# Seeding partial sums in PSUM by ScalarE copies in a two-layer Strassen-type matmul chain

## The chip, the cores and the metric

One core of a Trainium2 chip runs the whole program. The metric is device time in microseconds (us) of one execution; the kernel before takes 843.44 us (median of 3 runs, 843.13 to 844.32).

## What is computed

A decayed linear attention, then two feed-forward layers on the same 3072 tokens:

```python
for t in range(S):                                     # per batch b and head h, d = e = 64
    state = gamma * state + outer(k[t], v[t])
    y[t] = scale * q[t] @ state
x  = y.reshape(3072, 512)
x  = ((x @ w1) * (x @ w2)) @ w3 @ w_out                # w1, w2: 512x1024, w3: 1024x1024, w_out: 1024x512
x  = maximum(maximum(x @ w1', x @ w2'), x @ w3') @ w_out'   # w1' to w3': 512x768, w_out': 768x512
```

## The kernel before

The program has five stages, one behind the other, on TensorE (PE): attention (to 88 us), the products with w1 and w2 (called stage b here, 88 to 319 us), w3 merged with w_out and applied (to 494 us), the three products and their maximum (stage h, 494 to 760 us), and the last matrix. Its engines run instruction streams in a written order; nothing reorders them. VectorE is DVE, ScalarE ACT, GpSimd POOL, SyncE SP.

Stage b and stage h cut each matrix product into 2x2 quarters and form the four output quarters from seven products, q0 to q6, of summed quarters. Stage b runs 6 blocks: two groups `g` of weights times three blocks `n` of tokens (`blk = 3*g + n`). Stage h runs 9 blocks (`blk = 3*j + n`). In a block each product q makes GA = 4 (stage b) or GH = 3 (stage h) output pieces p, each of six matmuls into one PSUM bank of 512 columns. The seven products use two sets of banks, "a" and "b", by the table `ORDER`: q0 starts set a, q1 starts set b, q2 adds to a, q3 starts b anew, q4 adds to a, q5 adds to b, q6 adds to a. The sets change roles from block to block: set a of block n+1 is set b of block n.

After each piece its bank is read out (lines 494 to 511, 727 to 744): q0 is copied by ACT to the SBUF tile U, q1 is added to U by DVE, q2 and q3 are copied by ACT to C and E, q4 is subtracted from E by DVE, q5 subtracted from C by DVE and (stage b) multiplied with U on POOL, q6 multiplied with E (stage b) or put into a maximum (stage h). In stage h q1 gives m11: DVE adds the first piece into m11 (line 742), and for the other two adds to U and then takes the maximum with m11 (lines 742, 744).

Beside this run, ahead of the matmuls of a product:

- `op_split` (lines 241 and 242): the operand tile of a later product is rounded to a high part by ACT and gets its low part from DVE. In group 0 of stage b it is made two products ahead, from sums of quarters that `op_pre` (lines 255 to 261) forms on DVE three products ahead. In group 1 the tiles come back from DRAM by DMAs that ACT issues.
- `step`: the weights of the next group arrive as 64-bit numbers and are decoded in steps. A step alternates between `decode_a` (ACT line 117, POOL line 119, DVE lines 140, 142 and, of the piece before, line 134) and `decode_b` (ACT line 149, then a new fetch). `Spread` deals out the steps over the pieces, through `side.tick()` after each piece.
- `wgen` in the last block of a group: it makes the seven weight tiles of the next group (lines 204 to 214).

Of the kernel before, what the change touches and what calls it, by code (L numbers as in the profile page):

```python
# [12 lines left out]
ALU = mybir.AluOpType  # L13
# [19 lines left out]
GA = 4  # L33
# [14 lines left out]
def fused_kernel(ctx: ExitStack, tc: tile.TileContext, ck, w12, w3t, wo1, w123, wo2, mask, gout, gch, kdec, out):  # L48
    nc = tc.nc
# [119 lines left out]
    def store(dst, src, wait=1):  # L169
        later.append([wait, dst, src])  # L170
# [24 lines left out]
    def wslot(q, n=1024):  # L195
        return w_t[q][:, :2 * n].rearrange("p (h n) -> p h n", h=2)
# [55 lines left out]
    def op_pre(n, q, quad, quiet=False):  # L252
        t, sub = t_buf(n), ALU.subtract
        if q == 2:
            nc.vector.tensor_tensor(out=quad(0, 0), in0=quad(0, 1), in1=quad(0, 0), op=sub)
            nc.vector.tensor_tensor(out=t, in0=quad(1, 1), in1=quad(0, 0), op=sub)
        elif q == 3:
            eng = nc.vector if quiet else nc.gpsimd
            eng.tensor_tensor(out=quad(0, 1), in0=quad(1, 1), in1=quad(0, 1), op=sub)
        elif q == 5:  # L260
            nc.vector.tensor_tensor(out=t, in0=t, in1=quad(1, 0), op=sub)
# [106 lines left out]
    def quad_b(n):  # L368
        return lambda k, e: xr_t[n][:, 2 * k:2 * k + 2, e, :]
# [5 lines left out]
    with tc.manual_schedule():  # L375
# [23 lines left out]
        for _ in range(WARM):  # L399
# [7 lines left out]
        side = Spread([step] * (4 * GA) + [drain] + [job for q in (0, 1, 5, 2) for job in wgen.jobs(q)],  # L407
                      2 * (last - 3))
# [36 lines left out]
        for g in range(KF // GA):  # L445
            if g == 0:
                wq += [lambda i=i, u=u: fetch_w12(i, u) for i in range(GA, KF) for u in range(2)]
                more(3)
                side = Spread([idle] * 7 + [step] * (4 * GA), 2 * 28 + 4)
            else:  # L450
                x_st.close()
                m_st, m_pl = stage_pool("m")
                wo1_sb = [m_pl.tile([P, 2, 512], F32R, name=f"wo1_{k}") for k in range(KF)]
                w3_sb = [m_pl.tile([P, 2, 512], F32R, name=f"w3_{k}") for k in range(8)]
                w3_sb += [op_t[k // 2][:, :].rearrange("p (u h n) -> p u h n", u=2, h=2)[:, k % 2] for k in range(8)]
                wq += [lambda k=k: fetch(wo1[k], None, wo1_sb[k][:, 0], wo1_sb[k][:, 1]) for k in range(KF)]
                wq += [lambda k=k: fetch(w3t[k // 2, k % 2], None, w3_sb[k][:, 0], w3_sb[k][:, 1])
                       for k in range(2 * KF)]
                more(3)
                side = Spread([idle] * 3 + [step] * 32, 3 * 28)  # L460
            wgen = weights(raw_quads(1024), 1024)
            for n in range(NB):
                blk = g * NB + n
                sets = sets_b(blk)
                for q in range(7):
                    s = 7 * blk + q
                    if g == 0:
                        for d in (3, 2):
                            t = s + d
                            if t < 7 * NB:  # L470
                                qd = quad_b(t // 7)
                                if d == 3:
                                    op_pre(t // 7, t % 7, qd, quiet=True)
                                else:
                                    op_split(t, op_src(t // 7, t % 7, qd))
                                    store(opsp[t // 7, t % 7], op_t[t % 4].bitcast(F32))
                        if s < 2:
                            store(opsp[0, s], op_t[s].bitcast(F32))
                        for job in late_w.pop(s, ()):
                            job()  # L480
                    t = s + 3
                    if 7 * NB <= t < 14 * NB:
                        nc.scalar.dma_start(out=op_t[t % 4].bitcast(F32), in_=opsp[t // 7 - NB, t % 7])
                    which, first = ORDER[q]
                    x = op_slot(s)
                    w = wslot(q).rearrange("p h (i k n) -> p h i k n", i=GA, k=2)
                    for p in range(GA):
                        ps = sets[which][p]
                        for k in range(2):
                            wh, wl = w[:, 0, p, k, :], w[:, 1, p, k, :]  # L490
                            nc.tensor.matmul(ps, wh, x[:, 0, k, :], start=first and k == 0, stop=False, skip_group_check=True)  # L491
                            nc.tensor.matmul(ps, wh, x[:, 1, k, :], start=False, stop=False, skip_group_check=True)  # L492
                            nc.tensor.matmul(ps, wl, x[:, 0, k, :], start=False, stop=k == 1, skip_group_check=True)  # L493
                        u, c, e = (part(nm, p) for nm in "UCE")
                        if q == 0:
                            nc.scalar.copy(out=u, in_=ps)  # L496
                        elif q == 1:
                            nc.vector.tensor_tensor(out=u, in0=u, in1=ps, op=ALU.add)
                        elif q == 2:
                            nc.scalar.copy(out=c, in_=ps)  # L500
                        elif q == 3:
                            nc.scalar.copy(out=e, in_=ps)  # L502
                        elif q == 4:
                            nc.vector.tensor_tensor(out=e, in0=ps, in1=e, op=ALU.subtract)
                        elif q == 5:
                            nc.vector.tensor_tensor(out=c, in0=c, in1=ps, op=ALU.subtract)  # L506
                            nc.gpsimd.tensor_tensor(out=c, in0=c, in1=u, op=ALU.mult)  # L507
                            store(fsp[n, 0, :, g * GA + p, :], c, 1)
                        else:
                            nc.vector.tensor_tensor(out=e, in0=e, in1=ps, op=ALU.mult)  # L510
                            store(fsp[n, 1, :, g * GA + p, :], e, 0)
                        side.tick()
                    stores()
                    if g == 0 and n == NB - 1:
                        if q == 0:
                            side.rest()
                            drain()
                        wgen(q)
            side.rest()
# [149 lines left out]
        for j in range(GH):  # L669
# [16 lines left out]
            for n in range(NB):  # L686
# [3 lines left out]
                for q in range(7):  # L690
# [26 lines left out]
                    which, first = ORDER[q]  # L717
                    x = quads4(gen_t[s - held] if held <= s < held + len(gen_t) else op_t[s % 4])
                    w = wslot(q, 256 * GH).rearrange("p h (i k n) -> p h i k n", i=GH, k=2)
                    for p in range(GH):  # L720
                        ps = sets[which][p]
                        for k in range(2):
                            wh, wl = w[:, 0, p, k, :], w[:, 1, p, k, :]
                            nc.tensor.matmul(ps, wh, x[:, 0, k, :], start=first and k == 0, stop=False, skip_group_check=True)  # L724
                            nc.tensor.matmul(ps, wh, x[:, 1, k, :], start=False, stop=False, skip_group_check=True)  # L725
                            nc.tensor.matmul(ps, wl, x[:, 0, k, :], start=False, stop=k == 1, skip_group_check=True)  # L726
                        u, c, e = (part(nm, p) for nm in "UCE")
                        if q == 0:
                            nc.scalar.copy(out=u, in_=ps)
                        elif q == 2:  # L730
                            nc.scalar.copy(out=c, in_=ps)
                        elif q == 3:
                            nc.scalar.copy(out=e, in_=ps)
                        elif q == 6:
                            if p:
                                nc.vector.tensor_tensor(out=m12, in0=m12, in1=ps, op=ALU.max)
                            else:
                                nc.scalar.copy(out=m12, in_=ps)
                        else:
                            m, v, (x0, x1), op = {1: (m11, u, (u, ps), ALU.add), 4: (m22, e, (ps, e), ALU.subtract),  # L740
                                                  5: (m21, c, (c, ps), ALU.subtract)}[q]
                            nc.vector.tensor_tensor(out=v if p else m, in0=x0, in1=x1, op=op)
                            if p:
                                nc.vector.tensor_tensor(out=m, in0=m, in1=v, op=ALU.max)
                        side.tick()
# [117 lines left out]
```

## Time and profile before

| | |
|---|---|
| Median of 3 runs | 843.44 us |
| The profiled execution | 843.5 us, of which the span from first to last instruction is 841.7 us |
| Busy share of the span | PE 99%, DVE 70%, ACT 43%, POOL 14% |
| Instructions | PE 4720 matmuls, DVE 725, ACT 560, POOL 121 |
| TensorE clock granted | 1.000 of full speed |

A row of the timeline tells the start and length of one instruction (or of several alike in a row, with their number), and in brackets how long the engine had been idle and what it then waited for. A matmul row lasts 0.39 us, but the next one starts 0.23 us after it: matmuls overlap, so waits of PE are best read from starts. The group rows (by line) give number, total busy time, mean length in ns, and the idle time ahead of the group.

### The profile page before, as it was taken

Reading aid. Unit: us, or ns where it says so; the run is one execution under the profiler, and the core shown is the slowest. Engines: PE = TensorE matmul, PEld = TensorE weight load, DVE = VectorE, ACT = ScalarE, POOL = GpSimd, SP = SyncE. Lnnn points to the kernel's source line nnn. Section 1 sums busy time; section 2 is a strip of 40 time slices with the busy share of each in tenths; the row PEclk is TensorE's granted clock in tenths of the full one; section 3 lists DMA queues with packets and bytes.
Section 4 is the critical chain, followed back from the end, with each engine's and each line's share of the span. In section 5 each row is a group of like instructions: output and inputs, shape, how many; then the busy total and the mean of one; then the engine's idle time right before and its main releaser. Section 6 shows DMA issues by size and latency. Waiting matters only on the chain.

```text
span 841.7 us, 12200 instructions
## 1 busy us (share of the span) xinstructions
PE 830.0 (99%) x4720; PEld 694.1 (82%) x4720; DVE 589.0 (70%) x725; ACT 365.5 (43%) x560; POOL 120.8 (14%) x121
## 2 busy tenths in 40 slices
PE   8999999999999999999999999999999999999998
PEld 8889888878888888888888888887888888888886
DVE  3898978898475756753574657678657665878793
ACT  2544455354434343633555453343333334335542
POOL 3444031302031322100201000200000010000000
PEclk9999999999999999999999999999999999999999
DMA  9998367759988967462495699829998899856522
GB/s 347 408 406 337 152 283 289 288 213 369 362 324 312 340 228 263 150 218 87 147 336 213 218 410 412 334 88 382 409 361 300 318 367 357 291 239 228 209 101 75
DMA packets 54634, 235.00 MB, mean 279 GB/s; under 512 B 6320, under 2 KB 6448, under 8 KB 39344
## 3 DMA queue, kind: packets, MB, share of 16 engines
q1 hardware_dynamic: 37728, 133.46, 40.8%
q10 hardware_dynamic: 16848, 100.76, 32.5%
q8 instruction: 37, 0.61, 0.3%
q14 instruction: 21, 0.17, 0.1%
HBM read 161.85 MB, written 72.35 MB: 278 GB/s over the span
## 4 chain that ended last, share of the span: by engine, by line
PE 74%; DVE 3%; DMA 2%; issue 1%; ACT 0%; ACTq 0%; DVEq 0%
PE bank L724 9%; PE bank L725 9%; PE bank L726 9%; PE bank L492 5%; PE bank L601 5%; PE bank L603 5%; PE bank L493 5%; PE bank L602 5%; PE bank L491 5%; PE bank L783 3%; PE bank L784 3%; PE bank L782 3%; PE bank L540 2%; PE bank L542 2%; PE bank L541 2%; DMA opsp<-op 1%
## 5 line engine op out<-in xcount | busy, mean ns | idle before, releaser
L724 PE MATMUL bank<-op,w 128*128 128x512 f32 x360 | 140.1, 389 | 0.3 <-DMA op<-opsp 0.3
L725 PE MATMUL bank<-op,w 128*128 128x512 f32 x360 | 140.2, 389 | 0.2 <-DVE op L242 0.2
L726 PE MATMUL bank<-op,w 128*128 128x512 f32 x360 | 140.1, 389 | 0.0
L491 PE MATMUL bank<-op,w 128*128 128x512 f32 x336 | 130.9, 390 | 1.0 <-DVE E L510 1.0
L492 PE MATMUL bank<-op,w 128*128 128x512 f32 x336 | 130.9, 390 | 1.0 <-DVE op L242 1.0
L493 PE MATMUL bank<-op,w 128*128 128x512 f32 x336 | 130.7, 389 | 0.0
L119 POOL TENSOR_SCALAR dec<-dec 128x512 f32<-128x512 f32 x64 | 47.5, 742 | 481.6 <-ACT dec L117 457.2
L724 PEld LDWEIGHTS bank<-op,w 128*128 128x128 f32 x360 | 67.6, 188 | 14.8 <-issue 0.7
L725 PEld LDWEIGHTS bank<-op,w 128*128 128x128 f32 x360 | 67.6, 188 | 14.5 <-DVE op L242 0.6
L726 PEld LDWEIGHTS bank<-op,w 128*128 128x128 f32 x360 | 67.6, 188 | 14.1
L491 PEld LDWEIGHTS bank<-op,w 128*128 128x128 f32 x336 | 63.1, 188 | 14.7 <-ACT U L496 1.4
L492 PEld LDWEIGHTS bank<-op,w 128*128 128x128 f32 x336 | 63.1, 188 | 14.4 <-DVE op L242 1.7
L602 PE MATMUL bank<-op,w 128*128 128x512 f32 x192 | 74.7, 389 | 0.0
L601 PE MATMUL bank<-op,w 128*128 128x512 f32 x192 | 74.7, 389 | 0.0
L603 PE MATMUL bank<-op,w 128*128 128x512 f32 x192 | 74.7, 389 | 0.0
L493 PEld LDWEIGHTS bank<-op,w 128*128 128x128 f32 x336 | 63.1, 188 | 13.1
L149 ACT ACTIVATE dec<-stg 128x512 int32<-128x512 uint32 x59 | 39.6, 672 | 69.6 <-DVE stg L142 64.6
L117 ACT ACTIVATE dec<-stg 128x512 f32<-128x512 f32 x59 | 39.1, 663 | 30.3 <-DMA stg<-in_wo_dram 17.4
L140 DVE TENSOR_SCALAR dec<-dec 128x512 int32<-128x512 int32 x64 | 34.1, 533 | 23.0 <-POOL dec L119 23.0
L142 DVE SCALAR_TENSOR_TENSOR stg<-stg,dec 128x512 int32<-128x512 int32 x59 | 42.5, 720 | 5.2 <-ACT E L502 0.4
L507 POOL TENSOR_TENSOR C<-C,U 128x512 f32<-128x512 f32 x24 | 36.1, 1526 | 54.3 <-DVE C L506 54.2
L602 PEld LDWEIGHTS bank<-op,w 128*128 128x128 f32 x192 | 36.0, 188 | 7.5
(177 smaller groups left out, 1494.0 us busy)
## 6 DMA issues: line engine op xcount, KB each, us to landing
op<-opsp ACTq DMA_DIRECT2D x77, 1024.0 KB, 7.5
opsp<-op SPq DMA_DIRECT2D x25, 1024.0 KB, 5.0
ck<-in_ck_dram SPq DMA_DIRECT2D x48, 512.0 KB, 10.2
opsp<-w SPq DMA_DIRECT2D x14, 1024.0 KB, 5.9
stg<-in_w3t_dram ACTq DMA_DIRECT2D x16, 512.0 KB, 3.4
hsp<-m SPq DMA_DIRECT2D x32, 256.0 KB, 6.6
stg<-in_w_dram SPq DMA_DIRECT2D x15, 512.0 KB, 10.7
stg<-in_w_dram ACTq DMA_DIRECT2D x14, 512.0 KB, 5.1
```

The source lines that it names most:

```text
L119: nc.gpsimd.tensor_scalar(out=df, in0=df, scalar1=MAX_HI, scalar2=MIN_HI, op0=ALU.min, op1=ALU.max)
L142: nc.vector.scalar_tensor_tensor(out=top, in0=top, scalar=-0x40000000, in1=dec, op0=ALU.bitwise_and, op1=ALU.bitwise_or)
L149: nc.scalar.activation(out=dec, in_=low.bitcast(U32), func=ACT.Copy, scale=2.0 ** -29)
L491: nc.tensor.matmul(ps, wh, x[:, 0, k, :], start=first and k == 0, stop=False, skip_group_check=True)
L492: nc.tensor.matmul(ps, wh, x[:, 1, k, :], start=False, stop=False, skip_group_check=True)
L493: nc.tensor.matmul(ps, wl, x[:, 0, k, :], start=False, stop=k == 1, skip_group_check=True)
L601: nc.tensor.matmul(ps, wh, x[:, 0, k, :], start=kk == 0 and k == 0, stop=False)
L602: nc.tensor.matmul(ps, wh, x[:, 1, k, :], start=False, stop=False)
L603: nc.tensor.matmul(ps, wl, x[:, 0, k, :], start=False, stop=kk == 3 and k == 1)
L724: nc.tensor.matmul(ps, wh, x[:, 0, k, :], start=first and k == 0, stop=False, skip_group_check=True)
L725: nc.tensor.matmul(ps, wh, x[:, 1, k, :], start=False, stop=False, skip_group_check=True)
L726: nc.tensor.matmul(ps, wl, x[:, 0, k, :], start=False, stop=k == 1, skip_group_check=True)
```

## The change

In all blocks of stage b and stage h but the first one of each (44 pieces: 5 x 4 and 8 x 3), ACT copies the finished q0 piece into the bank of set b in place of U, and the q1 matmuls add to that bank (`start` is false for them). The sum q0 + q1 then stands in PSUM, and is read once: in stage b by an ACT copy to U, in stage h by an ACT copy to m11 (first piece) and by a DVE maximum (the other two). The 44 additions on DVE go.

In stage b the steps of the decode move: in group 0 the 16 steps are dealt over 22 pieces (the last two pieces of q3 and all of q4 in block 0, q1 to q4 in block 1, none in block 2), and in group 1 over the pieces of q1 to q6, so that none lies in q0. The sums for the third product of the next block (`op_pre(n + 1, 2)`, two DVE instructions) are formed in q5 instead of q6, ahead of that product's readouts. In stage h the steps stay where they were.

```diff
@@ stage b
-                side = Spread([idle] * 7 + [step] * (4 * GA), 2 * 28 + 4)
+                side = Spread([step] * (4 * GA), 22)
-                side = Spread([idle] * 3 + [step] * 32, 3 * 28)
+                side = Spread([idle] * 3 + [step] * 32, 3 * 24)
-                                if d == 3:
+                                if d == 3 and t % 7 != 2:
                                     op_pre(t // 7, t % 7, qd, quiet=True)
-                                else:
+                                elif d == 2:
                                     op_split(t, op_src(t // 7, t % 7, qd))
                                     store(opsp[t // 7, t % 7], op_t[t % 4].bitcast(F32))
+                                    if q == 5:
+                                        op_pre(n + 1, 2, quad_b(n + 1), quiet=True)
+                    seeded = blk > 0 and q == 1
-                            nc.tensor.matmul(ps, wh, x[:, 0, k, :], start=first and k == 0, stop=False, skip_group_check=True)
+                            nc.tensor.matmul(ps, wh, x[:, 0, k, :], start=first and k == 0 and not seeded, stop=False, skip_group_check=True)
                         if q == 0:
+                            nc.scalar.copy(out=sets["b"][p] if blk else u, in_=ps)
+                        elif seeded:
                             nc.scalar.copy(out=u, in_=ps)
                         elif q == 1:
                             nc.vector.tensor_tensor(out=u, in0=u, in1=ps, op=ALU.add)
-                        side.tick()
+                        if q if g else 4 * q + p in (range(14, 20), range(4, 20), ())[n]:
+                            side.tick()
@@ stage h
                         if q == 0:
-                            nc.scalar.copy(out=u, in_=ps)
+                            nc.scalar.copy(out=sets["b"][p] if blk else u, in_=ps)
-                        elif q == 6:
+                        elif seeded or q == 6:
+                            m = m12 if q == 6 else m11
                             if p:
-                                nc.vector.tensor_tensor(out=m12, in0=m12, in1=ps, op=ALU.max)
+                                nc.vector.tensor_tensor(out=m, in0=m, in1=ps, op=ALU.max)
                             else:
-                                nc.scalar.copy(out=m12, in_=ps)
+                                nc.scalar.copy(out=m, in_=ps)
```

Three places show what moves. The first is ACT in block 0 of stage b, products q3 and q4 (copies of E are q3's readout; L241 rounds an operand, L117 and L149 are the decode). Before:

```order
L241 CAST op_1101<-T 128x1024
L502 COPY E<-bank_1094 128x512
L502 COPY E<-bank_1095 128x512
L502 COPY E<-bank_1096 128x512
L502 COPY E<-bank_1097 128x512
L241 CAST op_1102<-xr_93 128x1024
L204 CAST w_71<-wraw 128x1024
L117 ACTIVATE dec_63<-stg_62 128x512
```

With the change:

```order
L241 CAST op_1101<-T 128x1024
L507 COPY E<-bank_1094 128x512
L507 COPY E<-bank_1095 128x512
L507 COPY E<-bank_1096 128x512
L117 ACTIVATE dec_63<-stg_62 128x512
L507 COPY E<-bank_1097 128x512
L149 ACTIVATE dec_63<-stg_62 128x512
L117 ACTIVATE dec_64<-stg_60 128x512
L241 CAST op_1102<-xr_93 128x1024
```

The first L149, which needs DVE's L142 of the same piece, now stands ahead of the rounding of op_1102.

The second is DVE in block 0, from the readout of q4 to that of q5 (E is q4's, C is q5's readout; xr_94 is the attention's output for block 1, L255 and L256 are `op_pre(1, 2)`). Before:

```order
L504 TENSOR_TENSOR E<-bank_1093,E 128x512
L242 TENSOR_TENSOR op_1103<-xr_94,op_1103 128x1024
L506 TENSOR_TENSOR C<-C,bank_1094 128x512
L506 TENSOR_TENSOR C<-C,bank_1095 128x512
L506 TENSOR_TENSOR C<-C,bank_1096 128x512
L506 TENSOR_TENSOR C<-C,bank_1097 128x512
L134 ISA wraw<-stg_62,dec_63 128x2x512
L140 TENSOR_SCALAR dec_64<-dec_64 128x512
L142 SCALAR_TENSOR_TENSOR stg_60<-stg_60,dec_64 128x512
L255 TENSOR_TENSOR xr_94<-xr_94 128x2x512
L256 TENSOR_TENSOR T<-xr_94 128x1024
```

With the change:

```order
L509 TENSOR_TENSOR E<-bank_1093,E 128x512
L134 ISA wraw<-stg_60,dec_64 128x2x512
L140 TENSOR_SCALAR dec_63<-dec_63 128x512
L142 SCALAR_TENSOR_TENSOR stg_61<-stg_61,dec_63 128x512
L242 TENSOR_TENSOR op_1103<-xr_94,op_1103 128x1024
L255 TENSOR_TENSOR xr_94<-xr_94 128x2x512
L256 TENSOR_TENSOR T<-xr_94 128x1024
L511 TENSOR_TENSOR C<-C,bank_1094 128x512
L511 TENSOR_TENSOR C<-C,bank_1095 128x512
L511 TENSOR_TENSOR C<-C,bank_1096 128x512
L511 TENSOR_TENSOR C<-C,bank_1097 128x512
```

The decode and the two sums of `op_pre` now stand ahead of the subtractions that read banks 1094 to 1097; these are set a of block 1.

The third is ACT at the start of block 1 of stage b (q0, then q1). Before:

```order
L241 CAST op_1101<-T 128x1024
L496 COPY U<-bank_1094 128x512
L496 COPY U<-bank_1095 128x512
L496 COPY U<-bank_1096 128x512
L496 COPY U<-bank_1097 128x512
L149 ACTIVATE dec_63<-stg_61 128x512
```

With the change:

```order
L241 CAST op_1101<-T 128x1024
L499 COPY bank_1090<-bank_1094 128x512
L499 COPY bank_1091<-bank_1095 128x512
L499 COPY bank_1092<-bank_1096 128x512
L499 COPY bank_1093<-bank_1097 128x512
L241 CAST op_1102<-xr_94 128x1024
L501 COPY U<-bank_1090 128x512
L149 ACTIVATE dec_63<-stg_61 128x512
```

The four copies now end in the banks that q1 adds to, and a second set of copies reads them out after q1.

## Rows read from the trace of the kernel before

**Rows 1.** Waits of PE from 88 us on: waiting line, releaser, total us, times, longest

```profile
PE bank L492 <- DVE op L242: 1.0, 1, 1.0
PE bank L491 <- DVE E L510: 1.0, 1, 1.0
PE bank L724 <- DMA op<-opsp: 0.3, 1, 0.3
PE bank L725 <- DVE op L242: 0.2, 1, 0.2
```

**Rows 2.** Timeline of PE: start of block 1, and the wait in block 2

```profile
126.48 0.39 PE L493 MATMUL bank<-op,w 128*128 128x512 f32 x1
126.71 0.39 PE L491 MATMUL bank<-op,w 128*128 128x512 f32 x1
...
187.88 0.39 PE L491 MATMUL bank<-op,w 128*128 128x512 f32 x1
189.30 0.50 PE L492 MATMUL bank<-op,w 128*128 128x512 f32 x1 [1.03 <-DVE op L242]
189.64 0.40 PE L493 MATMUL bank<-op,w 128*128 128x512 f32 x1
```

**Rows 3.** Timeline of DVE from 164 to 189 us, blocks 1 and 2

```profile
164.94 1.95 DVE L255 TENSOR_TENSOR xr<-xr 128x1024 f32<-128x1024 f32 x1
166.92 2.20 DVE L256 TENSOR_TENSOR T<-xr 128x1024 f32<-128x1024 f32 x1
...
180.98 2.47 DVE L498 TENSOR_TENSOR U<-U,bank 128x512 f32<-128x512 f32 x4
...
188.03 1.22 DVE L242 TENSOR_TENSOR op<-xr,op 128x1024 fp32r<-128x1024 f32 x1
```

**Rows 4.** Timeline of DVE in block 2 of stage h

```profile
559.48 0.68 DVE L742 TENSOR_TENSOR m<-U,bank 128x512 f32<-128x512 f32 x1
...
562.72 0.95 DVE L205 TENSOR_TENSOR w<-wraw_h,w 128x768 fp32r<-128x768 f32 x1
```

**Rows 5.** Timeline of ACT in block 0 of stage b, products q3 and q4

```profile
109.28 2.04 ACT L502 COPY E<-bank 128x512 f32<-128x512 f32 x4
...
113.08 0.70 ACT L117 ACTIVATE dec<-stg 128x512 f32<-128x512 f32 x1
...
117.60 0.68 ACT L149 ACTIVATE dec<-stg 128x512 int32<-128x512 uint32 x1 [2.88 <-DVE stg L142]
...
118.75 1.04 ACT L241 CAST op<-xr 128x1024 fp32r<-128x1024 f32 x1
```

**Rows 6.** Timeline of POOL in blocks 0 and 1: two clamps of the decode

```profile
113.87 1.26 POOL L119 TENSOR_SCALAR dec<-dec 128x512 f32<-128x512 f32 x1 [33.35 <-ACT dec L117]
...
138.40 0.61 POOL L119 TENSOR_SCALAR dec<-dec 128x512 f32<-128x512 f32 x1 [8.73 <-ACT dec L117]
```

**Rows 7.** Timeline of DVE in block 0 and at the start of block 1

```profile
112.30 1.22 DVE L242 TENSOR_TENSOR op<-xr,op 128x1024 fp32r<-128x1024 f32 x1 [1.67 <-ACT op L241]
...
114.57 1.88 DVE L504 TENSOR_TENSOR E<-bank,E 128x512 f32<-128x512 f32 x3
...
126.72 1.21 DVE L255 TENSOR_TENSOR xr<-xr 128x1024 f32<-128x1024 f32 x1
127.96 1.23 DVE L256 TENSOR_TENSOR T<-xr 128x1024 f32<-128x1024 f32 x1
...
135.32 0.68 DVE L134 CUSTOM_DVE_ANT_0 wraw<-stg,dec 128x1024 uint16<-128x1024 uint16 x1
...
136.38 0.69 DVE L142 SCALAR_TENSOR_TENSOR stg<-stg,dec 128x512 int32<-128x512 int32 x1
```

**Rows 8.** Groups by line, shapes apart: ACT copies out of PSUM, and ACT in SBUF

```profile
L729 ACT COPY U<-bank 128x512 f32<-128x512 f32 x27 | 15.5, 587 | 24.0 <-PE bank L726 22.1 <-DVE m L736 1.7
L351 ACT COPY st<-abank 64x256 f32<-64x256 f32 x40 | 14.7, 366 | 25.2 <-PE abank L347 24.5
L117 ACT ACTIVATE dec<-stg 128x512 f32<-128x512 f32 x59 | 39.1, 663 | 30.3 <-DMA stg<-in_wo_dram 17.4 <-DMA stg<-in_w3t_dram 9.3 <-DMA stg<-in_w_dram 3.2
```

More of the change, by code (lines that the diff above doesn't have):

```diff
@@ L719, in fused_kernel @@
                     w = wslot(q, 256 * GH).rearrange("p h (i k n) -> p h i k n", i=GH, k=2)
+                    seeded = blk > 0 and q == 1
                     for p in range(GH):
@@ L723, in fused_kernel @@
                             wh, wl = w[:, 0, p, k, :], w[:, 1, p, k, :]
-                            nc.tensor.matmul(ps, wh, x[:, 0, k, :], start=first and k == 0, stop=False, skip_group_check=True)
+                            nc.tensor.matmul(ps, wh, x[:, 0, k, :], start=first and k == 0 and not seeded, stop=False, skip_group_check=True)
                             nc.tensor.matmul(ps, wh, x[:, 1, k, :], start=False, stop=False, skip_group_check=True)
```

## The prediction, made before the changed kernel ran

> **What bounds the kernel now.** I read three things in this order. First the waits of TensorE (PE) from the end of attention on: the reader is to see how little there is to win. PE waits four times in 750 us, 2.5 us in all [rows 1]. Everything else there is PE working through matmuls that start 0.23 us apart [rows 2], and the change removes, adds and lengthens no matmul. Second, what one such wait costs beyond its listed length. The one in block 2 is listed with 1.03, but the start comes 1.42 after the one before instead of 0.23, and the next one takes 0.34 instead of 0.23 [rows 2]: 1.19 + 0.11 = 1.30, thus 0.27 more than listed. The four waits together: 2.5 + 4 x 0.27 = 3.6 us. That is the most that the change can win. Third, the timelines of DVE and ACT around the places where the diff moves work, because three of the four waits end with DVE and the moved work could make new ones.
>
> The sum is made against the profiled execution, 843.5 us, which is the median of the runs (843.44) within 0.1. A measurement can tell about 0.2%, or 1.7 us, from no change.
>
> **The additions that go.** 44 DVE additions leave, each about 0.6 (four in 2.47 [rows 3]). They lie beside matmuls, so they are worth only what they take off a wait.
> - Block 2, 1.30 us: PE waits for the low part (L242) that starts at 188.03 and so ends at 189.25, 0.05 before PE goes on [rows 2, 3]. The four additions ahead of it on DVE are 2.47, more than the 1.03 of the wait. I count it as gone.
> - Start of block 2, 1.0 + 0.27: PE waits for the bank that L510 reads out [rows 1]. Now a copy of 0.59 must follow L510 before PE may go on, so DVE has to be 1.6 us earlier. It saves the four additions of block 1, 2.47, and 1.7 on the two sums of `op_pre`: they took 1.95 and 2.20 [rows 3] against 1.21 and 1.23 in block 0 [rows 7], and are now ahead of the POOL multiplications of q5 instead of beside them. That makes 4.2 against 1.6: gone.
> - Stage h, block 2, 0.2 + 0.27 (low part) and 0.3 + 0.27 (a tile's DMA) [rows 1]. From 559.48 to 562.72 DVE takes 3.24 for five instructions [rows 4]; two maxima of about 0.65 are left, 1.9 less. The low part comes 1.9 earlier, and with it the store that the DMA's tile slot waits for. Both gone, the second less surely, since it passes through two DMAs.
>
> Sum: -3.6 us.
>
> **The copies.** The seeding copy goes from PSUM to PSUM, which no row shows. Below it is bounded by 0.37 (a quarter of the elements) and above by 0.66 (SBUF to SBUF); I take 0.59, that of the PSUM copy of the same shape [rows 8], which is nearest. PE wants the seeded bank three pieces of 6 x 0.23 after the q0 piece in stage b, two in stage h: less the 0.16 by which a matmul's record outlasts the next start, 3.9 and 2.6 us. So a copy may begin 3.3 or 2.0 late for nothing. The old copies in stage h found ACT free: 22.1 of the 24.0 us idle before them were spent on PE [rows 8]. The 28 new copies in q1 are 28 x 0.59 = 17 us of an engine that is busy 43%; what queues behind them is the rounding of an operand needed two products (11 us) later. Both at nothing, hidden by matmuls.
>
> **The moved decode and `op_pre` in block 0: a new wait.** Here I follow the streams. ACT's three copies of q3 take 0.48 apiece from 109.28 [rows 5], then L117 begins at 110.7. POOL follows 0.79 later (113.08 to 113.87 [rows 5, 6]), at 111.5; its clamp is 0.61 or 1.26 [rows 6], the short one where DVE is idle as here: 112.1. DVE's L140 and L142 take 0.45 and 0.69 [rows 7]: 113.25. Only then L149, L117 (1.15 together) and the rounding (1.04) run on ACT [rows 5]: 115.45. So the low part that started at 112.30 starts at 115.5, and the readout of q4 at 117.8 instead of 114.57 [rows 7], 3.2 later. From there to the end of the first C subtraction DVE has four q4 readouts (0.6 each, 2.4), two more decode steps with L134 (1.06 up to L142, and 0.69: 3.5), a low part 1.13, the two sums 1.24 and 1.23 [rows 7], and the subtraction 0.68: 10.2, so 128.0. Its bank is the first of set a of block 1, and PE wants it at 126.71 [rows 2]. Before, these subtractions stood ahead of decode and sums. PE waits 128.0 + 0.05 - 126.71 = 1.3, and 0.11 after: **+1.4 us**. Bounds: nothing, if DVE is 1.3 faster; and 1.4 + 2.0 = 3.4, if each of the three clamps takes the long 1.26. I take the short clamp, since DVE waits for it.
>
> Behind it: the other three subtractions 1.8, a low part 1.2 to 1.6, L515 0.68, then the seeding copy 0.59 end at 132.7; the bank is wanted at 126.71 + 1.4 + 5.4 = 133.5. So no second wait, with 0.8 to spare. POOL's multiplications and the stores on SP behind them move back some 8 us; their tile is overwritten only in q2 of the next block, and the next stage alone reads the stores.
>
> **Group 1 of stage b.** Its 35 slots come in 72 pieces instead of 84, none in q0. The fetches and DMA issues on ACT keep their number, and no wait of PE stands there now: nothing.
>
> **Sum:** 843.5 - 3.6 + 1.4 = **841.3 us**, with 840.2 to 842.5 for the case itself.
>
> **A rule against the trace.** L255 and L256 are 1.7 us longer in block 1, where POOL multiplies, than in block 0 [rows 3, 7]. The Trainium skill ("SBUF — State Buffer", Who interferes with whom) says that VectorE and GpSimd share a port pair as an exclusive lock, that a VectorE instruction with two SBUF inputs and a GpSimd one that reads SBUF block each other for a whole instruction, and that one SBUF input does not. The trace agrees in kind: these are two-input sums, and they are stretched. By the rule at its worst the decode steps moved into block 0 and POOL's clamps would hold each other up, and the sum would be 843.3 instead of 841.3; that is the second rival.
>
> **The rivals.**
> - *All four waits go and no new one comes*: 843.5 - 3.6 = 839.9. For it: DVE needs to be only 1.3 us faster over 17 us than I added up, and L142 may overlap its neighbour. Against: the chain through ACT has no slack. Chance 0.18.
> - *The block 0 chain is longer*: the clamps on POOL and the two-input instructions on DVE hold each other up, three times 0.65 (1.26 - 0.61 [rows 6]). The new wait is 3.4 and the time 843.3, no change. For it: one of the two clamps shown took the long time. Against: two of the three run while DVE waits. The lock named above would be its mechanism. Chance 0.12.
> - *The change does less than it says*: the DMA wait and one DVE wait stay, since ACT is now what the low parts wait for; 0.6 + 1.3 less won, 843.2. Chance 0.10.
> - *Slower: the seeding copies come late in stage h*, where the decode stays in q0. A decode L149 ahead of a copy can wait for DVE, 2.88 in one row [rows 5]; beyond 2.0 PE waits, 0.9 each. In all eight seeded blocks 7 us: 841.3 + 7 = 848. It turns the sign from 3.9 us in all, that is from five such blocks. Against: the 22.1 of 24.0 us above. Chance 0.10.
>
> **How the numbers follow.** The forecast has 0.50. Faster (under 841.8): 0.7 of the forecast, the first rival, and a little of the third: 0.55. Slower: the last, 0.10. The same: the remaining 0.35. The range from 839.6 to 843.4 takes in all but the slower rival and the tails, some 0.18.
>
> **What would show it.** PE's waits for op L242 and for L510 in block 2 and both in stage h gone; one wait near 126.7 for a C subtraction (the old L506), of about 1.3; the new copies about 0.59 long and PE never waiting for one; DVE busy shorter by 44 x 0.6 = 26 us. I am wrong if PE waits on ACT at the start of q1, if the start of block 1 shows no wait, or more than 2.6 us.

## The result, and the profile after

The changed kernel takes **848.82 us** (median of 5 runs, 848.09 to 849.93) against 843.44 of the kernel before (5 runs, 843.04 to 844.32). The ratio is 1.0064, with a 95% interval of 1.0049 to 1.0078: 5.4 us slower, where 2.1 us faster was forecast and the range ended at 843.4.

The page of the changed kernel: its span, and the busy time of each engine with its share and number of instructions.

```profile
span 847.3 us, 12187 instructions
...
PE 832.0 (98%) x4720; PEld 695.0 (82%) x4720; DVE 560.2 (66%) x681; ACT 381.7 (45%) x588; POOL 116.3 (14%) x121
```

DVE was busy 589.0 us before, so 28.8 us of work left it, and 44 instructions. That gained nothing. The waits of PE from 87 us on (waiting line, releaser, total us, times, longest) show where the time went:

```profile
PE bank L494 <- DVE C L511: 3.8, 2, 2.5
PE bank L494 <- DVE E L509: 2.3, 1, 2.3
...
PE bank L791 <- DVE w L673: 0.2, 1, 0.2
```

The four waits of before [rows 1] are gone, and three longer ones are there, 6.1 us instead of 2.5. The timeline of PE at these places:

```profile
128.09 0.47 PE L494 MATMUL bank<-op,w 128*128 128x512 f32 x1 [1.31 <-DVE C L511]
...
163.27 0.47 PE L494 MATMUL bank<-op,w 128*128 128x512 f32 x1 [2.28 <-DVE E L509]
...
171.54 0.47 PE L494 MATMUL bank<-op,w 128*128 128x512 f32 x1 [2.48 <-DVE C L511]
...
172.90 0.63 PE L496 MATMUL bank<-op,w 128*128 128x512 f32 x1
173.32 0.63 PE L494 MATMUL bank<-op,w 128*128 128x512 f32 x1
...
175.88 0.47 PE L494 MATMUL bank<-op,w 128*128 128x512 f32 x1
```

The first wait, at the start of block 1, is the one that was forecast. The second is in the last product (q6) of block 1, the third at the first matmul of block 2, where q0 needs a bank of the q5 readout. Behind the third, matmuls start 0.43 us apart instead of 0.23; the view of stretches gives the granted clock there as 0.62 (the third number from the end, ahead of the DMA share and GB/s; the mean of a stretch that holds matmuls at both levels of the clock, 1.2 and 2.4 GHz; from 172.9 to 175.9 us alone it is 0.50, the lower one):

```profile
171.50:176.00 4.50, 4.46 (x13) 3.53 (x14) 4.50 (x6) 0.65 (x2) 4.50 (x3) 0.62 0.31 117
```

By starts, each taken against the 0.23 us of an undisturbed matmul: 1.55 at 128 us, 2.52 at 163, 2.72 at 171.5, about 1.6 for the eight slow matmuls, and 1.1 in four small places. Together 9.5 us of late starts, against 3.8 in the kernel before. The difference, 5.7, is the difference of the spans (847.3 - 841.7 = 5.6), so these places account for all of the loss.

**What is late.** The chain goes back from PE to a DMA. First DVE:

```profile
161.29 1.23 DVE L242 TENSOR_TENSOR op<-xr,op 128x1024 fp32r<-128x1024 f32 x1 [5.06 <-ACT op L241]
162.44 1.28 DVE L509 TENSOR_TENSOR E<-bank,E 128x512 f32<-128x512 f32 x2
...
167.06 1.22 DVE L242 TENSOR_TENSOR op<-xr,op 128x1024 fp32r<-128x1024 f32 x1 [0.48 <-ACT op L241]
168.31 1.23 DVE L255 TENSOR_TENSOR xr<-xr 128x1024 f32<-128x1024 f32 x1
169.57 1.23 DVE L256 TENSOR_TENSOR T<-xr 128x1024 f32<-128x1024 f32 x1
170.72 1.88 DVE L511 TENSOR_TENSOR C<-C,bank 128x512 f32<-128x512 f32 x3
```

DVE, the engine that had been relieved, stands for 5.06 us and waits for ACT's rounding (L241); the readouts of q4 (L509) and of q5 (L511) stand behind it. Then ACT. L117 is the first instruction of a piece's decode. In these rows it runs at the end of the step before, behind that step's L149 and ahead of L86, which is the fetch of the next weight piece, issued by ACT:

```profile
140.12 0.33 ACTq L86 DMA_DIRECT2D stg<-in_w_dram  x1
...
148.50 0.66 ACT L117 ACTIVATE dec<-stg 128x512 f32<-128x512 f32 x1 [2.77 <-DMA stg<-in_w_dram]
148.53 0.33 ACTq L86 DMA_DIRECT2D stg<-in_w_dram  x1
...
153.63 0.66 ACT L117 ACTIVATE dec<-stg 128x512 f32<-128x512 f32 x1 [1.51 <-DMA stg<-in_w_dram]
153.64 0.33 ACTq L86 DMA_DIRECT2D stg<-in_w_dram  x1
...
159.66 0.67 ACT L117 ACTIVATE dec<-stg 128x512 f32<-128x512 f32 x1 [2.73 <-DMA stg<-in_w_dram]
160.23 1.03 ACT L241 CAST op<-xr 128x1024 fp32r<-128x1024 f32 x1
```

Each L117 waits for the fetch that was issued just one pair of steps earlier: 140.12 to 148.50, 148.53 to 153.63, 153.64 to 159.66, thus 5.1 to 8.4 us from issue to use. The rounding that DVE waits for stands right behind the last of the three on ACT. In the kernel before, the same engine, block and lines:

```profile
137.19 0.33 ACTq L86 DMA_DIRECT2D stg<-in_w_dram  x1
...
143.99 0.67 ACT L117 ACTIVATE dec<-stg 128x512 f32<-128x512 f32 x1
...
149.10 0.34 ACTq L86 DMA_DIRECT2D stg<-in_w_dram  x1
149.59 0.66 ACT L117 ACTIVATE dec<-stg 128x512 f32<-128x512 f32 x1
```

There, too, a fetch is used one pair later, but that is 6.8 us later (137.19 to 143.99), and no L117 of block 1 waits. Before, 7 idle slots and 16 steps were dealt over 60 pieces: a pair of steps, and with it one weight fetch, every 2 x 60 / 23 = 5.2 pieces. A piece is 6 x 0.227 us, so that is a pair every 7.1 us. The change deals eleven steps over the sixteen pieces of q1 to q4 of block 1: a pair every 2.9 pieces, or about 4 us.

The fetches also land later than before. The view of L86 from 130 to 160 us gives the times from issue to landing of four fetches, before the change:

```profile
DMA to landing us min/median/max: 3.3/4.7/5.3
```

and with it:

```profile
DMA to landing us min/median/max: 4.5/5.5/8.3
```

So the lead became shorter and the landing longer. ACT was ready for the three pieces 5.6, 3.6 and 3.3 us after their fetches were issued (start of L117, less its wait, less the issue), and they landed after 8.3, 5.0 and 5.9. At the 5.3 us of before the first wait, of 2.77, would not have come. And a late fetch makes the next one late: L86 stands behind the L117 that waits, and is issued at 148.53 and 153.64, right behind it.

### The profile page after: what moved, and what is told of

It is laid out like the page before. It is cut to its first block, busy times and chain, and to the rows that moved or that the text cites. A ratio compares the mean times of both kernels' runs of the same rounds, so it can differ in the third digit from the quotient of the medians.

```text
span 847.3 us, 12187 instructions
## 1 busy us (share of the span) xinstructions
PE 832.0 (98%) x4720; PEld 695.0 (82%) x4720; DVE 560.2 (66%) x681; ACT 381.7 (45%) x588; POOL 116.3 (14%) x121
## 4 chain that ended last, share of the span: by engine, by line
PE 77%; DVE 2%; issue 1%; ACT 0%; DVEq 0%
PE bank L731 10%; PE bank L733 10%; PE bank L732 10%; PE bank L494 6%; PE bank L496 6%; PE bank L495 6%; PE bank L607 5%; PE bank L609 5%; PE bank L608 5%; PE bank L791 3%; PE bank L792 3%; PE bank L790 3%; PE bank L547 2%; PE bank L546 2%; PE bank L548 2%
## 5 line engine op out<-in xcount | busy, mean ns | idle before, releaser
L494 PE MATMUL bank<-op,w 128*128 128x512 f32 x336 | 131.8, 392 | 6.1 <-DVE C L511 3.8
L119 POOL TENSOR_SCALAR dec<-dec 128x512 f32<-128x512 f32 x64 | 44.4, 694 | 488.6 <-ACT dec L117 462.1
L494 PEld LDWEIGHTS bank<-op,w 128*128 128x128 f32 x336 | 63.5, 189 | 21.0 <-issue 7.4
L149 ACT ACTIVATE dec<-stg 128x512 int32<-128x512 uint32 x59 | 39.5, 670 | 52.2 <-DVE stg L142 48.3
L117 ACT ACTIVATE dec<-stg 128x512 f32<-128x512 f32 x59 | 39.1, 663 | 22.1 <-DMA stg<-in_w_dram 9.8
L142 DVE SCALAR_TENSOR_TENSOR stg<-stg,dec 128x512 int32<-128x512 int32 x59 | 43.2, 732 | 4.9 <-DVE dec L140 0.5
```

The costliest lines, as they stand in the source:

```text
L119: nc.gpsimd.tensor_scalar(out=df, in0=df, scalar1=MAX_HI, scalar2=MIN_HI, op0=ALU.min, op1=ALU.max)
L142: nc.vector.scalar_tensor_tensor(out=top, in0=top, scalar=-0x40000000, in1=dec, op0=ALU.bitwise_and, op1=ALU.bitwise_or)
L149: nc.scalar.activation(out=dec, in_=low.bitcast(U32), func=ACT.Copy, scale=2.0 ** -29)
```

## The experiments

Three theories stood against each other. **F** (fetches): the block 1 steps come faster than their fetches land, and ACT, which executes in order, holds the rounding behind its wait. **S** (seeds): the copies into PSUM, or the `op_pre` moved with them, hold PE up. **D** (DMA): the stores that the change pushes together make each fetch land later. In the profiled execution of every kernel below, its time less the late starts of PE is 839.6 to 840.2 us, so the waits of PE account for all the differences. All ratios are against runs of the kernel before on the same chip (medians 843.44 to 843.48), with 95% intervals; rows with a wait of "L494" and the like carry each kernel's own line numbers.

### The decode of group 0 dealt as before

```diff
-                side = Spread([step] * (4 * GA), 22)
+                side = Spread([idle] * 7 + [step] * (4 * GA), 2 * 28 + 4)
-                        if q if g else 4 * q + p in (range(14, 20), range(4, 20), ())[n]:
+                        if q or not g:
```

> The change, with the decode steps of group 0 dealt out as before (16 steps over blocks 0 to 2, in q0 too); seeds, op_pre in q5 and group 1 as in the change. Theory F (fetch): in block 1 the change asks for a decoded pair every 2.9 pieces (3.9 us), while a fetch is issued one pair ahead and lands 5 to 8 us later; ACT waits for it and holds the operand roundings. Then with 7 us a pair both waits of 2.4 and 2.6 us around 163 and 171 us and the slow clock behind them go, and the 1.5 us at 128 us too: about 840 us. Theory S (seeds): the seeding copies, which wait on ACT for DVE's readouts, hold ACT up; then the waits stay, 846 us or more. Theory D (stores): the late C subtractions of block 0 hold SP's queue and the stores then crowd the fetches; since op_pre stays in q5 but no decode stands ahead, about 841.

Measured: 841.6 us (10 runs, 840.64 to 842.92), ratio 0.9977 [0.9968, 0.9986]. The three waits are gone, with nothing else undone; what is left of PE's waits is

```profile
PE bank L494 <- ACT bank L499: 1.2, 2, 1.0
...
PE bank L791 <- DVE w L673: 0.2, 1, 0.2
```

This dealing is worth 7.2 us. It speaks for F, or for any theory in which the early steps do harm. The time is 1.6 us above what F expected; 1.3 of it is a new late start at 286 us, which comes back below.

### `op_pre` back in q6

```diff
-                                if d == 3 and t % 7 != 2:
+                                if d == 3:
-                                elif d == 2:
+                                else:
-                                    if q == 5:
-                                        op_pre(n + 1, 2, quad_b(n + 1), quiet=True)
```

> The change, with op_pre for the next block back in q6, behind the C subtractions. F: the wait at 128 us goes (the subtraction ends 2.4 us earlier), the waits for fetches on ACT stay, so PE still waits about 2.4 us in q6 of block 1, and the start of block 2 loses its 2.6 us and the slow clock: about 843 us. S: the same as the change or 1.5 better, 847. D: subtractions and stores come earlier, the fetches land in time, and both later waits go: 841 us.

Measured: 848.74 us (4 runs, 846.27 to 850.03), ratio 1.0056 [1.0038, 1.0074]. I had expected a gain, and there was none. The wait of 1.5 at 128 us did go, but here PE waits for seeding copies, twice. DVE, ACT and PE at the first of them:

```profile
127.65 2.00 DVE L255 TENSOR_TENSOR xr<-xr 128x1024 f32<-128x1024 f32 x1
129.68 2.20 DVE L256 TENSOR_TENSOR T<-xr 128x1024 f32<-128x1024 f32 x1
131.80 2.31 DVE L242 TENSOR_TENSOR op<-xr,op 128x1024 fp32r<-128x1024 f32 x1
134.03 2.47 DVE L513 TENSOR_TENSOR E<-E,bank 128x512 f32<-128x512 f32 x4
```

```profile
134.80 2.36 ACT L497 COPY bank<-bank 128x512 f32<-128x512 f32 x4 [1.78 <-DVE E L513]
```

```profile
135.42 0.50 PE L492 MATMUL bank<-op,w 128*128 128x512 f32 x1 [2.71 <-ACT bank L497]
```

The two sums and the low part take 6.5 us beside POOL's multiplications (on POOL from 126.03 to 133.03) where, with `op_pre` in q5, the sums took 1.23 and 1.22. They stand ahead of the readout that frees the seeded bank. ACT waits for fetches here too, but 3.9 us instead of 7.0 (they land within 6.2), and the wait in q6 that I had expected to stay did not come. In the medians it all comes out even: with the move of `op_pre` PE is late by 1.5 at 128 us, and these two waits for copies don't come. My expectation that it could be undone for a gain fell.

### The moves without the seeds

The kernel before, with the decode and `op_pre` where the change puts them, and DVE's 44 additions kept:

```diff
-                side = Spread([idle] * 7 + [step] * (4 * GA), 2 * 28 + 4)
+                side = Spread([step] * (4 * GA), 22)
...
+                                    if q == 5:
+                                        op_pre(n + 1, 2, quad_b(n + 1), quiet=True)
...
-                        side.tick()
+                        if q if g else 4 * q + p in (range(14, 20), range(4, 20), ())[n]:
+                            side.tick()
```

> The kernel before, with the decode steps and op_pre moved as in the change, and no seeds anywhere. F: the late fetches stay and DVE has four additions more in each block, so it is as slow as the change or slower: 848 to 852 us. S: the waits of block 1 go: about 843. D: as F.

Measured: 849.51 us (4 runs, 849.04 to 851.01), ratio 1.0072 [1.0056, 1.0087]. The three waits are there without a single seeding copy, and ACT's 6.7 us in three waits for fetches too:

```profile
PE bank L493 <- DVE C L508: 3.9, 2, 2.5
PE bank L493 <- DVE E L506: 3.1, 1, 3.1
```

The slow matmuls come again behind the last one (late by 2.65 at 172.92). S falls as an explanation of this change.

### A fourth staging buffer

All as in the change, but weights are fetched one piece further ahead, into a fourth buffer that group 0 alone uses:

```diff
-        st = stg[k % NSTG][:, :] if st is None else st
+        st = ring[0][k % len(ring[0])][:, :] if st is None else st
-                more(3)
+                e_st, e_pl = stage_pool("e", "right")
+                ring[0] = stg + [e_pl.tile([P, 1024], F32, name="stg3")]
+                more(4)
```

> The change, with a fourth staging buffer for the weight fetches in group 0, so that a fetch has two pairs (7.9 us) instead of one; the order on DVE, POOL and SP stays. F: ACT's waits for fetches in block 1 (7 us) shrink to 1 or none, the PE waits at 163 and 171 us and the slow clock go (-6.7), the 1.5 us at 128 us stays: about 842 us. S: no difference, 848 to 849. D: the crowded DMA rings make the fetches as late with four buffers, at most 2 us better: 846 or more.

Measured: 842.22 us (10 runs, 841.88 to 844.07), ratio 0.9988 [0.9979, 0.9998]. The steps, their order and the stores are those of the change. On ACT:

```profile
145.33 0.34 ACTq L86 DMA_DIRECT2D stg<-in_w_dram  x1
145.81 0.66 ACT L117 ACTIVATE dec<-stg 128x512 f32<-128x512 f32 x1
...
149.30 0.71 ACT L117 ACTIVATE dec<-stg 128x512 f32<-128x512 f32 x1
...
153.77 0.66 ACT L117 ACTIVATE dec<-stg 128x512 f32<-128x512 f32 x1 [1.13 <-DMA stg<-in_w_dram]
154.34 1.04 ACT L241 CAST op<-xr 128x1024 fp32r<-128x1024 f32 x1
```

A fetch is now used two pairs later: the one issued at 145.33 by the L117 at 153.77. It took 8.4 us to land, no less than the slowest of the change, and still cost ACT only 1.13. Three waits of 7.0 us became this one, the rounding that was at 160.23 is at 154.34, and of PE's large waits only the one at 128 us is left (late by 1.54). This experiment names the cause: a fetch was issued too short a time before its use. More lead takes away 6.6 us, with the steps as early as in the change and fetches that land no sooner.

What makes the fetches land later is less clear. The seeds alone don't (5.4 us at most, in the run of that name below). In the change three stores of operands, of 1 MB each, were issued within 2.1 us (136.63 to 138.75) and took 6.7 to 10.7 us to land; the same three stores of the kernel before were issued over 7.0 us (133.57 to 140.54) and took 4.4 to 5.8. The DMA engines were fuller in the change (share 1.03 and 425 GB/s from 138.9 to 149.8 us, against 0.81 and 298 from 137.6 to 148.5 before). But with the decode dealt as before, and these stores nearly where they were, fetches took up to 7.2 us as well, and ACT waited 1.4 us for two of them. So the stores fit as a part of the cause, as D has it, but no run took them away, and their part isn't shown.

### The eleven steps over 24 pieces

Three buffers again; block 1's steps run on through q5 and q6.

```diff
-                side = Spread([step] * (4 * GA), 22)
+                late11 = [step if -(-11 * (t + 1) // 24) > -(-11 * t // 24) else idle for t in range(24)]
+                side = Spread([step] * 3 + [idle] + [step] * 2 + late11, 30)
-                        if q if g else 4 * q + p in (range(14, 20), range(4, 20), ())[n]:
+                        if q if g else 4 * q + p in (range(14, 20), range(4, 28), ())[n]:
```

> The change with three staging buffers, its five steps in block 0 kept, but the eleven steps of block 1 dealt over 24 pieces (q1 to q6) instead of 16: a pair every 4.4 pieces, 5.9 us, where the change asks for one every 3.9 us. F: fetches land 5 to 8 us after issue, so ACT's waits for them in block 1 fall from 7.0 to 3 us or less, and no operand's low part comes late: the PE waits of 2.4 and 2.6 us and the slow clock go; 1.5 us at 128 us stays, decode beside POOL in q5 and q6 may cost some tenths at the start of block 2: 842 to 843.5 us. If the number of steps in block 1 or the seeds, not their pace, make the waits: 847 or more.

Measured: 844.3 us (10 runs, 843.72 to 845.06), ratio 1.001 [1.0001, 1.002]: 4.5 us better than the change, and above the 842 to 843.5 that F expected. F had also expected ACT's waits for fetches to fall to 3 us or less, and there it was wrong: they are 6.6 us in three times, nearly as long as in the change. A pair every 5.9 us leaves more than any fetch of block 1 took in the kernel before (5.3), but here they took up to 8.4:

```profile
149.37 0.66 ACT L117 ACTIVATE dec<-stg 128x512 f32<-128x512 f32 x1 [1.91 <-DMA stg<-in_w_dram]
...
151.36 1.07 ACT L241 CAST op<-xr 128x1024 fp32r<-128x1024 f32 x1
...
156.27 0.68 ACT L117 ACTIVATE dec<-stg 128x512 f32<-128x512 f32 x1 [3.26 <-DMA stg<-in_w_dram]
```

```profile
DMA to landing us min/median/max: 4.5/5.7/8.4
```

ACT was ready for the first of these pieces 6.6 us after its fetch was issued. So the pace of the steps alone doesn't make these waits; the longer landing is needed for them. But only the first of the three stands ahead of the rounding that q4's readout needs. That rounding runs at 151.36 instead of 160.23, the readout begins at 153.61 instead of 162.44, and PE doesn't wait in q6; what is left is 1.6 us at 128, 0.7 in q1 of block 2 and 1.4 at 760 (each with the matmul behind). So not the length of ACT's waits sets the price, but what stands behind them in ACT's order.

### The seeds alone, and in stage h alone

The kernel before with the diff's lines on seeds and with nothing moved; then with those of stage h only.

> The kernel before with the seeds alone: decode in both groups and op_pre as before. F (fetch): no decode is crowded, so no wait for fetches on ACT; seeds take DVE's waits of before away, but op_pre in q6 runs beside the POOL multiplications, so L510 ends late and the seeding copy behind it makes PE wait up to 1 us at the start of q1 in blocks 1 and 2 of stage b: 842 to 843.5 us. S (seeds): the seeding copies cost more than the additions saved: 844 to 846.

Measured: 841.96 us (10 runs, 840.9 to 843.81), ratio 0.9983 [0.9974, 0.9992].

> The kernel before with the seeds of stage h alone. Both theories: the two waits of stage h (0.46 and 0.55 us) go and nothing else, about 842.4 us; stage b keeps its two waits of 1.3 us.

Measured: 842.82 us (10 runs, 842.54 to 843.82), ratio 0.9993 [0.9984, 1.0002]. The seeds alone do most of what I had forecast for the whole change. Of their 1.5 us about 0.6 come in stage h, where the interval still holds no gain, and the rest in stage b. With the seeds alone the wait for the low part in block 2 is gone. In q1 of block 2 the late start of 1.26 us (with the matmul behind it), which the prediction calls the start of block 2, gives way to one of 0.61 two pieces later, where PE waits for a seeding copy.

### A version that beats both

The kernel with the fourth buffer, with four decode steps in block 0 instead of five, to take away the 1.5 at 128 us:

```diff
-                side = Spread([step] * (4 * GA), 22)
+                side = Spread([step] * (4 * GA), 20)
-                        if q if g else 4 * q + p in (range(14, 20), range(4, 20), ())[n]:
+                        if q if g else 4 * q + p in (range(14, 18), range(4, 20), ())[n]:
```

> Four staging buffers as in e4, and in block 0 only four decode steps (over four pieces) instead of five, so that one decode on DVE less (1.75 us) stands ahead of the C subtractions. F: the wait at 128 us (1.5) goes too, the fetches still come in time with 12 steps in block 1: about 840.7 us. If the start of block 1 waits for something else than the C subtraction, 842 as e4.

Measured: 842.87 us (11 runs, 841.64 to 844.0), ratio 0.9991 [0.9982, 0.9999]. That wait did fall, from 1.54 to 0.29 late, but the time didn't: in the profiled execution (844.0 us, the slowest of the eleven) others came at 166 us (0.75), 287 and 761. That at 287 is a seeding copy held on ACT, by a DMA issue that stands ahead of it:

```profile
286.39 0.33 ACTq L489 DMA_DIRECT2D op<-opsp  x1
286.76 1.55 ACT L503 COPY bank<-bank 128x512 f32<-128x512 f32 x3 [2.03 <-DMA fsp<-C]
```

In group 1, q0 begins with the issue of an operand load, and that waits until a store has landed; the copies are queued behind it. So the load of q0 is issued behind the copies instead:

```diff
-                    if 7 * NB <= t < 14 * NB:
+                    if 7 * NB <= t < 14 * NB and q:
...
+                    if 7 * NB <= t < 14 * NB and not q:
+                        nc.scalar.dma_start(out=op_t[t % 4].bitcast(F32), in_=opsp[t // 7 - NB, t % 7])
```

> As e7, and in group 1 of stage b ACT issues the operand load of q0 behind the four seeding copies instead of ahead of them. e1 showed one seeding copy in block 5 held by a load issued ahead of it (PE waited 1.2 us there), e4 and the change 0.1 to 0.2. If that varies from run to run: 840.5, and less scatter than e7; else as e7.

Measured: 841.2 us (7 runs, 840.72 to 842.41), ratio 0.9975 [0.9965, 0.9986], where 840.5 was expected. At 287 us PE no longer waits. The same edit on the first experiment (decode dealt as before), where PE was late by 1.19 at 286.39 for the same reason:

> e1 (seeds, op_pre in q5, group 0 decoded at the pace of before) with the operand load of q0 in group 1 issued behind the seeding copies. F: e1's remaining waits are 0.45 us in block 2, 1.3 us in block 5 (the load ahead of the copies) and 0.4 us at the last stage; the 1.3 goes: 840.5 us, the fastest so far. Else as e1, 841.6.

Measured: **840.28 us** (5 runs, 840.17 to 841.09), ratio 0.9964 [0.9951, 0.9976]: 3.2 us less than the kernel before and 8.5 less than the change, with no new buffer. In the profiled execution (841.09 us, the slowest of the five) PE is late by 1.4 us in all, and its waits are

```profile
PE bank L494 <- ACT bank L499: 0.4, 1, 0.4
PE bank L793 <- DVE w L675: 0.2, 1, 0.2
```

## Why the prediction was wrong, point by point

- *The additions that go, -3.6*: right for the waits, somewhat too large for the gain. All four waits are gone, and DVE is 28.8 us less busy (forecast 26). But with the seeds alone the median falls by 1.5, and 0.61 us of lateness stays in q1 of block 2. In stage h a start 0.30 us late at 598 came in the place of 1.0.
- *The copies, nothing*: right for this kernel. They take 0.573 us (forecast 0.59, PSUM to SBUF 0.586):

```profile
L736 ACT COPY bank<-bank 128x512 f32<-128x512 f32 x24 | 13.7, 573 | 24.6 <-PE bank L733 22.9 <-DVE m L744 1.5 <-ACT dec L117 0.3
...
L499 ACT COPY bank<-bank 128x512 f32<-128x512 f32 x20 | 11.1, 573 | 14.1 <-DVE E L515 7.7 <-PE bank L496 5.5 <-DMA fsp<-C 0.8
```

  In the change PE is held by one only at 293 us, late by 0.23 with the matmul behind. It waited for them in the variants (late by 1.19 and 1.33 at 286 to 287 us, 2.87 and 3.35 with `op_pre` in q6, 0.3 to 0.6 in q1 of block 2 in four kernels), so "hidden by matmuls" held by the order of ACT and DVE around it, not by the length of the copy.
- *The new wait in block 0, +1.4*: right. The first C subtraction was forecast to end at 128.0 and PE to be late by 1.4; the row below begins its four at 127.27, and PE is late by 1.55 with the matmul behind. The clamps on POOL took the short 0.61, as chosen, so the second rival, that they and DVE hold each other up, did not come.

```profile
127.27 2.47 DVE L511 TENSOR_TENSOR C<-C,bank 128x512 f32<-128x512 f32 x4
```

- ***The start of block 2, "That makes 4.2 against 1.6: gone"*: this is the step that failed.** It balanced DVE's busy time in block 1, and left out that eleven decode steps now stood in that block, each pair with a fetch. I followed the moved steps through block 0 instruction by instruction, but for block 1 neither the price of the steps nor their DMAs got a term, and the lead of a fetch was never held against the time that it takes to land. DVE was to be 4.2 us earlier; it stood 5.06 us waiting for ACT, and ACT for fetches. The runs put in its place: late by 2.72 at the first matmul of block 2, 2.52 in q6 of block 1, and 1.6 for slow matmuls behind, 6.8 us together. Giving the fetch more lead (fourth buffer) takes away 6.6, dealing the steps as before 7.2. The two sums of `op_pre` did take 1.23 apiece, as forecast: that gain on DVE was real, and lost in the wait for ACT. The one wait that this step speaks of, for the bank of L510 in q1 of block 2, is not there in the change; but PE came there 5.2 us late already, so that proves little. Without the late fetches 0.45 us (decode as before) or nothing (fourth buffer) is left there.
- *"POOL's multiplications and the stores on SP behind them move back some 8 us"*: seen, and costed at nothing because nobody waits for the stores. What the stores meet in the DMA queues, the fetches, was not asked. The fetches did land later (4.5 to 8.3 us against 3.3 to 5.3); that these stores are the reason is not shown.
- *The rivals*: none named a fetch. The slower rival had the right shape, ACT held up by a decode step that waits, but put it in stage h, with DVE as what it waits for, and with the seeding copies as its victim. Here it is in stage b, the wait is for a DMA, the victim is a rounding, and it comes without seeds too. The bound for being wrong, a wait of more than 2.6 us at the start of block 1, was not what happened: that wait was as forecast, and the loss came from q6 of that block on.

Three things stay open. The first is what lengthened the fetches. The second is why late starts at 758 to 768 us (last stage, waits for DVE's L673 and its like) differ between profiled executions, 0.07 to 1.36 us. The third is why q1's start near 287 us (293 in the change) is late by 1.2 or 1.3 us in two kernels and by 0.2 us or less in others with the same code there. In these two the store of C whose landing the load waits for took 7.7 and 7.8 us to land, in the change, with `op_pre` in q6, with four buffers and over 24 pieces 5.9 to 6.6; why it took longer is not known.

## What to carry to other kernels

When work that carries a prefetch is moved or dealt more densely, compare the time from a fetch's issue to its use with the time from its issue to its landing, at the place where it will run and beside the stores that will run there. On an engine that executes in order, a wait for a load costs what stands behind it: look for the instruction that another engine needs, and keep it ahead of the load's first user. Busy time taken off an engine, 28.8 us here, says nothing of the end: the same seeds gave 5.4 us more or 3.2 us less than before, by where the decode steps and a load stood in ACT's order around them.

## What the runs showed of the hardware

- After a wait of PE its matmuls can be slow for a while. In the change they started 0.43 us apart from 172.9 to 175.9 us, behind a start that was late by 2.64 (171.54), but not after the 2.44 at 163.27; with `op_pre` in q6, after 2.87 (135.42), granted clock 0.57 from 135.4 to 139.3 us, but not after 3.35 (178.59, granted clock 1.00 from 178.5 to 182), nor without the seeds after 3.28 (164.64). Some 1.6 us each time, and not foreseen. The length of the wait alone doesn't decide it; what does wasn't tried.
- A copy of 128x512 from PSUM to PSUM by ACT takes 0.573 us, 0.013 less than from PSUM to SBUF.
- A DVE sum with two SBUF operands of 128x1024 takes 1.2 us alone and 2.0 to 2.3 beside a POOL multiplication. The Trainium skill ("SBUF — State Buffer", Who interferes with whom) states the two engines' lock for this pair of instructions; the rows of the kernel before [rows 3] and those with `op_pre` in q6 agree in kind, and give the size.
